# Windowed attention into a mixture of experts on one core: copies of values in their own step, logits of step 13 in a slot's bank, no weight split in steps 10 and 11 and one more in step 13

## The chip, the cores and the metric

The kernel runs on one core of a Trainium2 chip. The metric is the time of one execution on the device in microseconds (us). Five engines work side by side: TensorE (PE, with its weight loads as PEld), VectorE (DVE), ScalarE (ACT), GpSimd (POOL) and SyncE (SP, which issues most DMAs). Each runs its own list of instructions in order; semaphores make one engine wait for another or for a DMA.

## The reference

The attention has 8 batches, 8 heads, 576 positions and 64 values per head, with a causal window of 64. Its output, 4608 rows of 512, goes through a mixture of 8 experts with one expert per row:

```python
scores = scale * np.matmul(q, k.transpose(0, 1, 3, 2))
mask = (rel >= 0) & (rel < 64)            # rel: position of the query less that of the key
attn = softmax(np.where(mask, scores, -1e9))
x = (attn @ v) as rows of 512             # 4608 rows
logits = x @ w_gate + modality_bias[modality_id]
e = argmax(logits); gate = softmax(logits)[e]
out[row] = gate * (relu(x[row] @ w1[e]) @ w2[e])      # w1: 512 x 1024, w2: 1024 x 512
```

Everything is fp32.

## The kernel before, in words

**Steps.** The 4608 rows are 36 pairs of 64-row blocks, 128 rows each. The main loop (line 983) has 36 + 4 steps `s`, and every pair goes through a pipeline of steps. The order of the work is written out by hand: the order of the code is the order of the instructions on every engine, and no scheduler moves anything. In step `s` stand, in this order: `values(s-2)` on PE (attention by values, L635, bank `av`) with `values_out` on DVE (L641 and L643, which makes the rows `xa`); `logits(s-3)` (PE L660 and the addition of the bias on DVE, L665); `scores(s)` (PE L583 into `sp`) with `minima(s)` on DVE (L597); `probs_t(s-1)`, which transposes the softmax on PE (L441) and copies it out on ACT (L618, `pT`); `sums` on POOL (L624); part of the exponentials of pair `s` on ACT (L609); `x_t(s-2)`, the transposition of `xa` (PE L441, then ACT); the heads' transpositions of the next group of queries and keys (`heads_t`, PE L441, copied by DVE or ACT at L548); and in odd steps from 5 on the routing of a group of two pairs (`route2`, `route3`). The routing ends in two scatters of rows on POOL (L736, `xs_scratch<-xa,idx`). While a scatter still reads `xa`, the five buffers of `xa` cannot be written.

**Values.** A pair needs its values twice: `vo` as loaded (SP L499, three buffers) and `ve`, in which the halves are shifted by 64 rows (two buffers). The upper half of `ve[p]` is copied from `vo[p-1]` by DVE (`swap_upper`, L513), the lower half from `vo[p]` by POOL (`swap_v`, L507). Both copies for pair `s-1` are made in step `s`. `values(s-1)` in step `s+1` reads them.

**Experts.** From step `FIRST` = 12 on, work of the mixture of experts is set into the attention: a `gap` is a place in a step at which some matmuls of a slot (256 rows of one expert) are issued. A step has four of them: `first(k, i)` (L280: 12 matmuls into a bank `em` or `sp0`, for the `i`-th half of hidden block `k`) and `second(k, t)` (L302: six matmuls into `y0` or `y1`). Step 12 has a slot's rows and `first(0,0)` and `first(0,1)`; step 13 has `first(1,0)`, `first(1,1)`, `second(0,0)`, `second(0,1)`; step 14 has `first(2,0)`, `first(2,1)`, `second(1,0)`, `second(1,1)`; and so on. After `first(k,1)` ACT makes `hh` (L288) and DVE `hl` (L289), the two parts of the hidden values.

**Weights.** Every matmul of the experts is three: high part by high part, high by low, low by high. The weights of two experts come in 32 pieces of 128 x 512. A call of `weights(s)` (L971) does three things: DVE makes the low part `Wlo` of the piece whose high part was made in the call before (L117), ACT makes the high part `Whi` of the oldest loaded piece (L112), and SP issues the load of another piece (L101 or L105) into one of four buffers `y`. So the low part of the piece with number `n` in the order of the pieces is made three calls after the load, and each call stands in its place of the step. The order is `PIECE_ORDER = (0, 2, 4, 6, 8, 9, 1, 3, 5, 7, 10, ...)`: pieces 0, 2, 4, 6 are what `first(0, .)` and `first(1, .)` need, 8 and 9 what `second(0, .)` needs, 1, 3, 5, 7 the rest of `w1`, 10 and 11 (numbers 10 and 11 in the order) what `second(1, .)` needs. Here `lo3` means the low part of number 3 in the order, and so on. One call stands at the end of each step from `WEIGHTS` = 5 on (L1067). There are two calls more in step 12 (L1041 ahead of `first(0,0)`, and L1056) and in steps 13 to 15 (L1033 and L1056), later one more in odd steps. Nothing but the place in the code and the semaphores keeps a matmul behind its low part; `ready` (L196) refuses only a wrong order of the code.

**Banks.** Transpositions and logits take a PSUM bank from a rotation (`turn_bank`, L485). Before step 12 it has five banks, from then on only the two of `tp`, which are shared by everything that is transposed. The logits of step 12 have bank `y0`, which is still free there (L999).

Of the kernel before, what the change touches and what calls it, by code (L numbers as in the profile page):

```python
# [8 lines left out]
F32 = mybir.dt.float32  # L9
# [10 lines left out]
P = 128  # L20
# [6 lines left out]
def tile_window_attn_moe(  # L27
# [13 lines left out]
    B, H, S, D = q.shape  # L41
# [7 lines left out]
    NPR = NBLK // 2  # L49
# [13 lines left out]
             (12, (0, 2)), (13, (0, 2)), (15, (0, 2)))  # L63
    WEIGHTS = 5
    FIRST = 12


    LATE = ((0, False), (1, True), (0, False), (1, True), (0, True), (1, True))
# [28 lines left out]
    def load_piece(raw, ev, c):  # L97

        if c * WCH < WC:
            ch, f0 = divmod(c * WCH, F)  # L100
            nc.sync.dma_start(  # L101
                out=raw, in_=w1_v[bass.ds(ev, 1), :, ch, f0:f0 + WCH].rearrange("o p f -> (o p) f"))
        else:
            c2 = c - WC // WCH
            nc.sync.dma_start(out=raw, in_=w2_v[bass.ds(ev, 1), :, c2, :].rearrange("o p f -> (o p) f"))  # L105
        return raw

    def split_hi(raw, buf, c):

        if Whi[buf] is None:  # L110
            Whi[buf] = wpool.tile([P, 2 * WC], F32R, name="Whi1")
        nc.scalar.copy(out=Whi[buf][:, c * WCH:(c + 1) * WCH], in_=raw)  # L112

    def split_lo(raw, buf, c):

        cols = slice(c * WCH, (c + 1) * WCH)
        nc.vector.tensor_tensor(  # L117
            out=Wlo[buf][:, cols], in0=raw, in1=Whi[buf][:, cols].bitcast(F32), op=ALU.subtract)
# [8 lines left out]
    def tick(n=1, table=False):  # L127
        for _ in range(n):
            if routing and not table:
                routing.pop(0)()  # L130
            elif queue:
                queue.pop(0)()
                issued[0] += 1
# [98 lines left out]
    def fetch():  # L232
        if fetched:
            return fetched.pop(0)
        row, late, buf, whichever, need = todo.pop(0)
        assert late is not None or not pads
        assert late is None or late in scattered
        tick(need - issued[0], table=True)
        nb = 1 if whichever == NANY else 2
        return dict(xt=load_slot(row, late, nb), buf=buf, any=whichever, nb=nb)  # L240
# [192 lines left out]
    def gap(it, wait=False):  # L433

        if next(it, "end") != "end" and not wait:
            run_later()
            tick()
# [10 lines left out]
    ps_m = actx.enter_context(tc.tile_pool(name="ps_m", bufs=1, space=PSUM))  # L448

    att = actx.enter_context(tc.tile_pool(name="att", bufs=1))  # L450
    work = actx.enter_context(tc.tile_pool(name="work", bufs=1))
# [12 lines left out]
    def by_group(x):  # L464
        return x.rearrange("p (a h j) i -> p a h j i", a=2, h=HP)
# [7 lines left out]
    ve = {}  # L473
# [11 lines left out]
    def turn_bank(s):  # L485

        i = n_tp[0]
        n_tp[0] += 1
        if s < FIRST and i % 5 > 1:
            return ps_m.tile([P, 512], F32, name=("em", "y0", "y1")[i % 5 - 2])  # L490
        return ps_t.tile([P, 512], F32, name="tp")

    def load_v(p):
# [6 lines left out]
        else:  # L500
            for i, g in enumerate((g0, g1)):
                s0 = (g % BPB) * W64
                nc.sync.dma_start(out=t[i * W64:(i + 1) * W64], in_=v_v[g // BPB, s0:s0 + W64])

    def swap_v(p):

        nc.gpsimd.tensor_copy(out=ve[p][0:W64], in_=vo[p][0:W64])  # L507

    def swap_upper(p):
        if p not in ve:  # L510
            ve[p] = work.tile([P, H, D], F32, name="ve", bufs=2)
        if p > 0:
            nc.vector.tensor_copy(out=ve[p][W64:P], in_=vo[p - 1][W64:P])  # L513

# [31 lines left out]
    def heads_out(tp, G, nm, i, copy):  # L546
        dst = by_group(qT if nm == "q" else kT)[:, G % 2, 2 * i:2 * i + 2]
        copy(out=dst.rearrange("p h j (i t) -> p h t (j i)", t=2),  # L548
             in_=tp.rearrange("p (h t i) -> p h t i", h=2, t=2))
# [104 lines left out]
    def logits(p, lt):  # L654
        G, j = divmod(p, GB)
        xaT = st.pop((p, "xT"))
        for c in range(NC1):
            for i in range(2):
                cols = slice(c * P + i * W64, c * P + (i + 1) * W64)
                nc.tensor.matmul(  # L660
                    out=lt[i * W64:(i + 1) * W64, 0:E], lhsT=xaT[:, cols], rhs=wg[:, c, :],
                    start=(c == 0), stop=(c == NC1 - 1))
        if j == 0:
            st[G, "lg"] = small.tile(sh3, F32, name="lg")
        nc.vector.tensor_tensor(  # L665
            out=st[G, "lg"][:, j, :], in0=lt[:, 0:E], in1=bias_sel[:, p, :], op=ALU.add)
# [144 lines left out]
    def when(step, f, *args):  # L811
        at.setdefault(max(step, -1), []).append((f, args))
# [6 lines left out]
    for p in range(NPR):  # L819
        when(p, load_v, p)  # L820
    when(FIRST - 1, lambda: fetched.append(fetch()))
    for G in range(1, NG):
# [148 lines left out]
    def weights(s):  # L971

        if halves:
            split_lo(*halves.pop(0))
        if len(raws) == 2 or raws and not pieces:
            split_hi(*raws[0])
            halves.append(raws.pop(0))
        while pieces and len(raws) < 2:
            x, c = pieces.pop(0)
            raw = epool.tile([P, WCH], F32, name="y", bufs=4)  # L980
            raws.append((load_piece(raw, evs[x], c), x, c))

    for s in range(NPR + 4):
        j = s % GB
        for f, args in at.pop(s, ()):
            f(*args)
        n_tick = 6 if s < FIRST else 5
        n_gap = 0 if s < FIRST else 4
        G = s // GB + 1
        heads = PARTS[j] if G < NG else ()  # L990
        R = (s - 5) // GB if s >= 5 and j == 1 else -1
        if 1 <= s < FIRST:
            swap_upper(s - 1)

        if 2 <= s < NPR + 2:
            values(s - 2)
            values_out(s - 2)
        if 3 <= s < NPR + 3:
            logits(s - 3, turn_bank(s) if s != FIRST else ps_m.tile([P, 512], F32, name="y0"))  # L999
            if (s - 3) % GB == GB - 1:  # L1000
                route1((s - 3) // GB)
        if s < NPR:
            scores(s)
            if s == FIRST:
                gap(it, True)
            minima(s)
            if s == FIRST - 2:
                tick(todo[0][-1] - issued[0], table=True)
        if 1 <= s <= NPR:
            if s == FIRST:  # L1010
                run_later()
            if s >= FIRST:
                swap_upper(s - 1)
            swap_v(s - 1)
            for a in range(2):
                probs_t(s - 1, a, turn_bank(s))
            sums(s - 1)
        if s < NPR:
            exps(s, (0, 1))
        if s == 0:  # L1020
            first_pair(1, (both[:1], both[1:]))
            cast_bias()
        if n_gap > 0 and s != FIRST:
            gap(it, True)
        if 2 <= s < NPR + 2:
            x_t(s - 2, turn_bank(s) if s != FIRST else ps_m.tile([P, 512], F32, name="y0"))
        run_later()
        tick(2)
        if s < NPR:
            exps(s, (2, 3, 4))  # L1030
        if n_gap > 0:
            if FIRST < s < FIRST + 4 or s % 2:
                weights(s)  # L1033
            if s != FIRST:
                gap(it, True)
        if heads:
            tp = turn_bank(s)
            heads_t(G, *heads[0], tp)
            heads_out(tp, G, *heads[0], nc.vector.tensor_copy)
        if s == FIRST:  # L1040
            weights(s)  # L1041
            gap(it, True)
        run_later()
        tick(n_tick)
        cnt = None
        if R >= 0:
            tp = turn_bank(s)
            rk = route2(R, tp)
            if R == NG - 1 or any(R == T for T, _ in EARLY):
                cnt = counts_out(tab if R == NG - 1 else pl, counts(R, tp))  # L1050
            route3(R, rk)
        if s < NPR:
            exps(s, (5, 6, 7))
        if n_gap > 2:
            if FIRST <= s < FIRST + 4:
                weights(s)  # L1056
            gap(it, True)
        if heads:
            tp = turn_bank(s)
            heads_t(G, *heads[1], tp)  # L1060
            heads_out(tp, G, *heads[1], nc.scalar.copy if heads[1] == K1 else nc.vector.tensor_copy)
        run_later()
        tick(n_tick)
        if s == WEIGHTS:
            load_weights()
        if s >= WEIGHTS:
            weights(s)  # L1067
        if n_gap > 3:
            gap(it, True)
        run_later()  # L1070
        if s == 1:
            select_bias()
        if s == 4:
            nc.sync.dma_start(out=xs_blk[DUMMY:DUMMY + 2].rearrange("b p c -> p b c"), in_=padrow)
        for T, xs_ in EARLY:
            if T == R:
                plan(T, xs_, cnt)
# [267 lines left out]
```

## Time and profile before

| | |
|---|---|
| three runs | 634.1, 636.05, 635.59 us |
| their median | 635.59 us |
| the profiled execution's own time | 635.35 us |
| its span | 633.6 us |
| mean granted clock of PE | 0.994 |

The span is the time from the first to the last instruction that the profile shows; the profiled execution's own time is 1.75 us longer. In the profile's lists of instructions a row gives start and duration in us, engine, line, operation, destination and sources (partitions x elements and type), the number of instructions that the row joins, and in brackets how long the engine had stood idle before and what ended that. The tables of waits give for each kind of wait the total in us, how often it occurred, and the longest one. The tables by stretches of time give for each stretch its length, then the busy time and count of PE, PEld, DVE, ACT and POOL.

### The profile page before, as it was taken

The numbers are of one execution on the slowest core, as the hardware profiler recorded it, in microseconds if no ns is written. First come the engines' busy times: TensorE is split into PE (matmuls) and PEld (weight loads), VectorE is DVE, ScalarE is ACT, GpSimd is POOL, SyncE is SP. The second block draws the span as 40 slices with busy tenths as digits, with TensorE's granted clock in tenths as the row PEclk, the third lists the DMA queues.
The fourth block names the chain that finished last, engine by engine and source line by source line (L and its number), as shares of the span: only waits on it lengthen the run. The fifth ranks groups of instructions, "written<-read, shape, count | busy, mean of one in ns | idle before, by whom it ended". The sixth has DMA issues, their size and how long they took to land.

```text
span 633.6 us, 17229 instructions
## 1 busy us (share of the span) xinstructions
PE 617.9 (98%) x6513; PEld 554.1 (87%) x6513; DVE 359.9 (57%) x1449; ACT 299.0 (47%) x933; POOL 136.0 (21%) x315
## 2 busy tenths in 40 slices
PE   8999899999999999999999999999999999999996
PEld 5888789889898889898988898999899989989886
DVE  3899987676777666656644353212314714666511
ACT  3899886757566646555462111111113513554411
POOL 6332412212320320322122221001001101101102
PEclk7999999999999999999999999999999999999999
DMA  9999856676457452544212117302332713677300
GB/s 181 206 245 229 226 143 200 169 185 185 131 141 199 134 151 61 148 136 112 68 52 101 62 73 285 96 21 68 86 114 90 247 64 124 199 242 250 99 8 30
DMA packets 138773, 88.07 MB, mean 139 GB/s; under 512 B 116618, under 2 KB 116672, under 8 KB 138560
## 3 DMA queue, kind: packets, MB, share of 16 engines
q1 hardware_dynamic: 130112, 67.44, 40.4%
q0 software_dynamic: 5888, 18.93, 7.8%
q8 instruction: 52, 0.85, 0.6%
q10 hardware_dynamic: 2688, 0.58, 0.4%
q14 instruction: 33, 0.27, 0.1%
HBM read 67.49 MB, written 23.91 MB: 144 GB/s over the span
## 4 chain that ended last, share of the span: by engine, by line
PE 64%; DVE 0%; ACT 0%; issue 0%; POOL 0%; POOLq 0%; ACTq 0%
PE y L302 26%; PE em L280 16%; PE sp L280 10%; PE tp L441 4%; PE av L635 2%; PE sp L583 2%; PE y L353 1%; PE tp L660 1%; PE em L255 1%; PE tp L255 1%; PE sp L328 0%; PE em L328 0%; DVE xa L643 0%; ACT ss L609 0%; POOL out_dram L366 0%
## 5 line engine op out<-in xcount | busy, mean ns | idle before, releaser
L302 PE MATMUL y<-Whi,hh 128*128 128x512 f32 x288 | 118.7, 412 | 0.0
L609 ACT ACTIVATE ss<-ss,mn 128x128 f32<-128x128 f32 x288 | 112.7, 398 | 2.9 <-DMA y<-in_moe_modality_id_dram 2.2
L302 PE MATMUL y<-Whi,hl 128*128 128x512 f32 x288 | 112.8, 392 | 0.0
L302 PE MATMUL y<-Wlo,hh 128*128 128x512 f32 x288 | 112.7, 391 | 0.0
L280 PE MATMUL em<-xh,Whi 128*128 128x256 f32 x400 | 102.8, 291 | 0.1
L280 PE MATMUL em<-xh,Wlo 128*128 128x256 f32 x400 | 98.0, 279 | 0.0
L289 DVE SCALAR_TENSOR_TENSOR hl<-em,hh 128x512 fp32r<-128x512 f32 x50 | 34.5, 689 | 91.0 <-ACT hh L288 91.0
L313 POOL DMA_INDIRECT out_dram<-y,id x36 | 37.3, 1037 | 221.4 <-DVE y L310 140.1
L280 PEld LDWEIGHTS em<-xh,Whi 128*128 128x128 f32 x400 | 75.4, 189 | 1.3 <-DVE xl L194 0.4
L280 PEld LDWEIGHTS em<-xh,Wlo 128*128 128x128 f32 x400 | 75.3, 188 | 0.9
L288 ACT ACTIVATE hh<-em 128x512 fp32r<-128x512 f32 x50 | 29.6, 592 | 92.8 <-PE em L280 88.8
L597 DVE CUSTOM_DVE_ANT_0 ss<-sp,masks 128x128 f32<-128x128 f32 x288 | 63.6, 285 | 11.3 <-PE sp L583 11.1
L618 ACT COPY pT<-tp 128x512 f32<-128x512 f32 x57 | 31.6, 591 | 72.5 <-PE tp L441 72.3
L302 PEld LDWEIGHTS y<-Whi,hl 128*128 128x128 f32 x288 | 54.1, 188 | 12.3
L280 PE MATMUL em<-xl,Whi 128*128 128x256 f32 x400 | 63.0, 279 | 0.0
L302 PEld LDWEIGHTS y<-Whi,hh 128*128 128x128 f32 x288 | 54.1, 188 | 7.3
L302 PEld LDWEIGHTS y<-Wlo,hh 128*128 128x128 f32 x288 | 54.3, 188 | 7.0
L609 ACT ACTIVATION_READ_ACCUMULATOR ss<-ss,mn 128x1 f32 x288 | 56.2, 195 | 0.0
L736 POOL DMA_INDIRECT xs_scratch<-xa,idx x36 | 36.3, 1009 | 83.1 <-DVE lm L679 27.2
L280 PEld LDWEIGHTS em<-xl,Whi 128*128 128x128 f32 x400 | 53.7, 188 | 0.0
L289 DVE SCALAR_TENSOR_TENSOR hl<-sp,hh 128x512 fp32r<-128x512 f32 x22 | 15.2, 691 | 60.8 <-ACT hh L288 60.8
L288 ACT ACTIVATE hh<-sp 128x512 fp32r<-128x512 f32 x22 | 13.1, 597 | 76.6 <-PE sp L280 76.6
(249 smaller groups left out, 1259.7 us busy)
## 6 DMA issues: line engine op xcount, KB each, us to landing
xt<-xs_scratch SPq DMA_DIRECT2D x18, 514.0 KB, 4.0
vo<-in_v_dram SPq DMA_DIRECT2D x32, 256.0 KB, 3.8
y<-in_moe_w_dram SPq DMA_DIRECT2D x32, 256.0 KB, 3.9
vo<-in_moe_w_dram SPq DMA_DIRECT2D x24, 256.0 KB, 3.7
ss<-in_moe_w_dram SPq DMA_DIRECT2D x24, 256.0 KB, 3.8
xs_scratch<-xs_scratch SPq DMA_DIRECT2D x8, 514.0 KB, 5.8
pT<-in_moe_w_dram SPq DMA_DIRECT2D x16, 256.0 KB, 3.6
qk<-in_k_dram SPq DMA_DIRECT2D x14, 256.0 KB, 5.0
```

The lines of the kernel that those rows point to most:

```text
L255: nc.tensor.transpose(out=tp[:, n * P:(n + 1) * P].bitcast(F32R), in_=xt[:, t, c * P:(c + 1) * P].bitcast(F32R), identity=ident_r)
L280: nc.tensor.matmul(out=hb[:, i * TP:(i + 1) * TP], lhsT=w[buf][:, c0:c0 + P], rhs=x[:, c * TP:(c + 1) * TP], start=(n == 0), stop=(n == le ...
L288: nc.scalar.activation(out=hh, in_=hb, func=AF.Relu),
L289: nc.vector.scalar_tensor_tensor(out=hl, in0=hb, scalar=0.0, in1=hh.bitcast(F32), op0=ALU.max, op1=ALU.subtract)))
L302: nc.tensor.matmul(out=sl["y", t], lhsT=h[:, i * TP + t * P:i * TP + (t + 1) * P], rhs=w[buf][:, c0:c0 + DM], start=(k == 0 and n == 0), s ...
L313: ins = nc.gpsimd.indirect_dma_start(out=out, out_offset=bass.IndirectOffsetOnAxis(ap=sl["id"][:, t:t + 1], axis=0), in_=y, in_offset=None ...
L441: nc.tensor.transpose(out=out_, in_=in_, identity=ident[p0:p0 + n, p0:p0 + n])
L583: nc.tensor.matmul(out=sp[a][c * W64:(c + 1) * W64, hp * P:(hp + 1) * P], lhsT=qT[rows, place(g + c, hp), :], rhs=kT[rows, win(c, hp), :], ...
L597: nc.vector.tensor_tensor_reduce(out=ss[a][:, hp, :], in0=sp[a][:, hp * P:(hp + 1) * P], in1=mask, scale=-1.0 / 8.0, scalar=3.0e38, op0=AL ...
L609: nc.scalar.activation(out=ss[a][:, hp, :], in_=ss[a][:, hp, :], func=AF.Exp, bias=mn[:, h:h + 1], scale=-1.0, accum_out=sm[:, h:h + 1])
L618: nc.scalar.copy(out=pT, in_=pp)
L736: ins = nc.gpsimd.indirect_dma_start(out=xs, out_offset=bass.IndirectOffsetOnAxis(ap=idx[:, j:j + 1], axis=0), in_=xg[j], in_offset=None)
```

## The change

There are three parts.

1. `swap_v` is moved. POOL's copy of the lower half of `ve[s]` now stands in step `s` itself, after the first half of the heads' transpositions and ahead of the routing; it was made in step `s+1` ahead of `probs_t`. `new_ve` allocates the buffer for whichever of the two copies comes first.
2. The logits of step 13 have the bank `y0`, too, instead of one of the two banks `tp`.
3. The calls of `weights` at the ends of steps 10 and 11 are left out (`PAUSE`). The call of step 12 ahead of `first(0,0)` now has its like in step 13, so step 13 has four calls. All pieces behind the third are made two calls later than before in steps 12 and 13, and one call later from the end of step 13 on; the last low part moves from step 25 to step 26.

```diff
@@ constants
     FIRST = 12
+    PAUSE = 10, 11
@@ values
-    def swap_v(p):
-
-        nc.gpsimd.tensor_copy(out=ve[p][0:W64], in_=vo[p][0:W64])
-
-    def swap_upper(p):
+    def new_ve(p):
         if p not in ve:
             ve[p] = work.tile([P, H, D], F32, name="ve", bufs=2)
+
+    def swap_v(p):
+
+        new_ve(p)
+        nc.gpsimd.tensor_copy(out=ve[p][0:W64], in_=vo[p][0:W64])
+
+    def swap_upper(p):
+        new_ve(p)
         if p > 0:
             nc.vector.tensor_copy(out=ve[p][W64:P], in_=vo[p - 1][W64:P])
@@ the main loop, step s
         if 3 <= s < NPR + 3:
-            logits(s - 3, turn_bank(s) if s != FIRST else ps_m.tile([P, 512], F32, name="y0"))
+            logits(s - 3, ps_m.tile([P, 512], F32, name="y0") if FIRST <= s < FIRST + 2 else turn_bank(s))
...
             if s >= FIRST:
                 swap_upper(s - 1)
-            swap_v(s - 1)
+            if s == 1:
+                swap_v(0)
             for a in range(2):
                 probs_t(s - 1, a, turn_bank(s))
...
             heads_out(tp, G, *heads[0], nc.vector.tensor_copy)
+        if FIRST <= s < FIRST + 2:
+            weights(s)
         if s == FIRST:
-            weights(s)
             gap(it, True)
         run_later()
         tick(n_tick)
+        if 1 <= s < NPR:
+            swap_v(s)
         cnt = None
...
-        if s >= WEIGHTS:
+        if s >= WEIGHTS and s not in PAUSE:
             weights(s)
```

On POOL, steps 5 and 6 before, from the copy for pair 4 on: the copy for pair 4, the sums of step 5, the two scatters of the routing in step 5, and then the copy for pair 5 and the sums of step 6.

```order
L507 COPY ve<-vo 64x512
L624 TENSOR_SCALAR rs<-sm 128x8
L735 COPY xa_101<-idc 128x1
L736 DMA xs_scratch<-xa_101,idx 39168x514
L735 COPY xa_102<-idc 128x1
L736 DMA xs_scratch<-xa_102,idx 39168x514
L507 COPY ve<-vo 64x512
L624 TENSOR_SCALAR rs<-sm 128x8
```

The same place after the change (all lines behind the new function are five higher):

```order
L513 COPY ve<-vo 64x512
L629 TENSOR_SCALAR rs<-sm 128x8
L513 COPY ve<-vo 64x512
L740 COPY xa_101<-idc 128x1
L741 DMA xs_scratch<-xa_101,idx 39168x514
L740 COPY xa_102<-idc 128x1
L741 DMA xs_scratch<-xa_102,idx 39168x514
L629 TENSOR_SCALAR rs<-sm 128x8
```

The copy for pair 5 has moved from behind the two scatters to ahead of them.

On PE, `first(0,0)` in step 12 before: four pairs of matmuls by the high and the low part of pieces 0, 2, 4, 6 (numbers 0 to 3), then four by the low part `xl` of the rows. A name with a number is one buffer; `Whi_65` and `Wlo_66` hold the parts of the first expert's weights.

```order
L280 MATMUL em<-xh,Whi_65 128x256 [waits DVE_49]
L280 MATMUL em<-xh,Wlo_66 128x256
L280 MATMUL em<-xh,Whi_65 128x256
L280 MATMUL em<-xh,Wlo_66 128x256
L280 MATMUL em<-xh,Whi_65 128x256
L280 MATMUL em<-xh,Wlo_66 128x256
L280 MATMUL em<-xh,Whi_65 128x256
L280 MATMUL em<-xh,Wlo_66 128x256
L280 MATMUL em<-xl,Whi_65 128x256 x2
L280 MATMUL em<-xl,Whi_65 128x256 [waits DVE_49]
L280 MATMUL em<-xl,Whi_65 128x256
```

The same matmuls after the change:

```order
L281 MATMUL em<-xh,Whi_65 128x256 [waits DVE_49]
L281 MATMUL em<-xh,Wlo_66 128x256
L281 MATMUL em<-xh,Whi_65 128x256
L281 MATMUL em<-xh,Wlo_66 128x256
L281 MATMUL em<-xh,Whi_65 128x256
L281 MATMUL em<-xh,Wlo_66 128x256
L281 MATMUL em<-xh,Whi_65 128x256
L281 MATMUL em<-xh,Wlo_66 128x256 [waits DVE_49]
L281 MATMUL em<-xl,Whi_65 128x256 x4
```

The order is the same; the eighth matmul, by `lo3`, now has a wait of its own for DVE, because `lo3` is made in step 12 itself. It was made at the end of step 10.

On PE, `second(1,0)` in step 14 before, six matmuls into one bank by the parts of pieces 10 and 11:

```order
L302 MATMUL y_2095<-Whi_65,hh 128x512
L302 MATMUL y_2095<-Wlo_66,hh 128x512
L302 MATMUL y_2095<-Whi_65,hl 128x512
L302 MATMUL y_2095<-Whi_65,hh 128x512
L302 MATMUL y_2095<-Wlo_66,hh 128x512 [waits DVE_49]
L302 MATMUL y_2095<-Whi_65,hl 128x512
```

The same six after the change:

```order
L303 MATMUL y_2093<-Whi_65,hh 128x512
L303 MATMUL y_2093<-Wlo_66,hh 128x512 [waits DVE_49]
L303 MATMUL y_2093<-Whi_65,hl 128x512
L303 MATMUL y_2093<-Whi_65,hh 128x512 [waits Activation_49]
L303 MATMUL y_2093<-Wlo_66,hh 128x512 [waits DVE_49]
L303 MATMUL y_2093<-Whi_65,hl 128x512
```

The order is the same again. The fifth matmul, by `lo11`, waited for the first call of step 14 (L1033) before; now it waits for the second one (L1056 before, `weights` ahead of the third gap), because `lo11` comes a call later. The second matmul waits for `lo10` of the first call and the fourth for ACT's high part of piece 11, made in that call.

More of the change, by code (lines that the diff above doesn't have):

```diff
@@ L503, in load_v @@
                 nc.sync.dma_start(out=t[i * W64:(i + 1) * W64], in_=v_v[g // BPB, s0:s0 + W64])
+    def new_ve(p):
+        if p not in ve:
+            ve[p] = work.tile([P, H, D], F32, name="ve", bufs=2)
     def swap_v(p):
+        new_ve(p)
         nc.gpsimd.tensor_copy(out=ve[p][0:W64], in_=vo[p][0:W64])
     def swap_upper(p):
-        if p not in ve:
-            ve[p] = work.tile([P, H, D], F32, name="ve", bufs=2)
+        new_ve(p)
         if p > 0:
```

## The prediction

> **What bounds the kernel now.** First the page: its first part for the engines, its second for where in the span they are busy.
>
> ```profile
> span 633.6 us, 17229 instructions
> PE 617.9 (98%) x6513; PEld 554.1 (87%) x6513; DVE 359.9 (57%) x1449; ACT 299.0 (47%) x933; POOL 136.0 (21%) x315
> PE   8999899999999999999999999999999999999996
> DVE  3899987676777666656644353212314714666511
> PEclk7999999999999999999999999999999999999999
> ```
>
> PE bounds the span: it is busy for 98% of it, and only 15.7 us (633.6 - 617.9) are left, part of them at the start and the end. The change adds no matmul and removes none, so it can gain only idle time of PE. The table of waits, PE's rows, names what there is:
>
> ```profile
> PE av L635 <- POOL ve L507: 2.5, 4, 0.8
> PE tp L441 <- DVE lg L665: 1.9, 3, 1.0
> PE tp L441 <- DVE xa L643: 1.5, 1, 1.5
> ```
>
> The three parts of the change aim at these three rows: 5.9 us together. But a wait that goes is a gain only if nothing else is late by then, and the second digit row shows DVE at 0.8 to 0.9 of its time in slices 2 to 5 (16 to 80 us). So I looked at what DVE waits for from step 4 to step 13, in the timeline and in one stretch:
>
> ```profile
> 31.63 0.29 DVE L597 CUSTOM_DVE_ANT_0 ss<-sp,masks 128x128 f32<-128x128 f32 x1 [0.24 <-PE sp L583]
> 46.60 0.69 DVE L643 TENSOR_TENSOR xa<-av,rs 128x512 f32<-128x512 f32 x1 [0.74 <-DMA xs_scratch<-xa,idx]
> 31.63:82.66 51.03, 46.84 (x865) 42.02 (x863) 48.15 (x269) 48.26 (x190) 18.72 (x36) 1.00 0.88 225
> ```
>
> In these 51 us DVE is busy for 48.15 us and ACT for 48.26 us, more than PE (46.84 us). Behind the 0.24 us on PE at 31.63 DVE's only longer wait is the 0.74 us on a scatter. Here DVE sets the pace, and PE's waits are what DVE leaves over.
>
> **Part 1, the copy of values.** The four waits of PE for POOL's copy:
>
> ```profile
> 23.99 0.27 PE L635 MATMUL av<-ve,pT 128*64 128x64 f32 x1 [0.83 <-POOL ve L507]
> 44.40 0.27 PE L635 MATMUL av<-ve,pT 128*64 128x64 f32 x1 [0.75 <-POOL ve L507]
> 55.05 0.27 PE L635 MATMUL av<-ve,pT 128*64 128x64 f32 x1 [0.46 <-POOL ve L507]
> 66.52 0.27 PE L635 MATMUL av<-ve,pT 128*64 128x64 f32 x1 [0.47 <-POOL ve L507]
> 36.91 0.23 POOL L624 TENSOR_SCALAR rs<-sm 128x8 f32<-128x8 f32 x1 [4.08 <-ACT ss L609]
> 41.15 1.10 POOL L736 DMA_INDIRECT xs_scratch<-xa,idx  x1 [3.76 <-issue]
> ```
>
> All four go: the copy no longer stands behind two scatters, and POOL has 3.76 us free ahead of them. The last three lie in the stretch of DVE; PE would only reach DVE's next product sooner, so I cost them at 0. The first one, in step 3, lies before it, where DVE waits for PE. Everything from there on comes up to 0.83 us earlier: bounds 0 and 0.83, taken 0.83.
>
> **Part 3, the steps without a split.** These are the rows around the end of step 11 and the start of step 12:
>
> ```profile
> 69.40 0.69 DVE L117 TENSOR_TENSOR Wlo<-y,Whi 128x512 fp32r<-128x512 f32 x1
> 70.13 0.42 DVE L513 COPY ve<-vo 64x512 f32<-64x512 f32 x1
> 71.62 0.65 PE L441 MATMUL tp<-ident_r,xa 128*128 128x128 f32 x4 [1.47 <-DVE xa L643]
> 75.33 1.10 PE L583 MATMUL sp<-kT,qT 64*64 64x128 f32 x32
> 75.12 0.68 DVE L117 TENSOR_TENSOR Wlo<-y,Whi 128x512 fp32r<-128x512 f32 x1
> 75.72 0.19 DVE L641 RECIPROCAL rs<-rs 128x8 f32<-128x8 f32 x1
> 80.25 0.28 PE L280 MATMUL em<-xh,Wlo 128*128 128x256 f32 x1
> 81.35 0.68 DVE L117 TENSOR_TENSOR Wlo<-y,Whi 128x512 fp32r<-128x512 f32 x1
> ```
>
> Two splits leave DVE ahead of step 12: 70.13 - 69.40 = 0.73 and 75.72 - 75.12 = 0.60 us. With part 1, DVE is 0.83 + 0.73 = 1.56 us earlier by the scores of step 12, which start at 73.77 in place of 75.33, and 0.83 + 0.73 + 0.60 = 2.16 us earlier by its own list behind them. The minima can't run ahead of the scores, so between 1.56 and 2.16 I take 1.65.
>
> But a new wait stands there. The eighth matmul of `first(0,0)` needs `lo3`, which was made in step 10; now the first split of step 12 makes it, at the place of the row 81.35. It starts at 81.35 - 1.65 = 79.70 and ends at 80.38, and PE follows at about 80.45. Before, this matmul ran at 80.25. So the gain of 1.65 us that PE brings into step 12 is used up there, and 0.2 us more: **+0.2 by the eighth matmul**, whatever came before. (If part 1 brings nothing in step 3, DVE is 0.83 later, and it is +1.0.)
>
> **Part 2, the logits of step 13.** The transpositions of `probs_t` in step 13:
>
> ```profile
> 85.31 0.66 PE L441 MATMUL tp<-ident_r,ss 128*128 128x128 f32 x4
> 86.93 0.66 PE L441 MATMUL tp<-ident_r,ss 128*128 128x128 f32 x4 [0.97 <-DVE lg L665]
> 87.34 0.36 PE L280 MATMUL em<-xh,Whi 128*128 128x256 f32 x1
> ```
>
> From the first four to `first(1,0)` it is 87.34 - 85.31 = 2.03 us. Without the logits in a `tp` bank the second four follow the first directly. Four of them hold PE until the next instruction for 87.34 - 86.93 = 0.41 us, so eight take 0.82, say 0.85 us: a gain of 1.18. Its bounds are 0.97, the wait itself, and 1.2. No other reader of a `tp` bank is late there by the timeline. **-1.2**, so that PE stands at 0.2 - 1.2 = -1.0 from step 13 on. The extra split of step 13 (0.68 us of DVE) lies in waits of DVE for PE of 1 us.
>
> **Part 3 again, in step 14.** The fifth matmul of `second(1,0)` needs `lo11`, which the first call of step 14 made; now the second call does.
>
> ```profile
> 99.66 0.68 DVE L117 TENSOR_TENSOR Wlo<-y,Whi 128x512 fp32r<-128x512 f32 x1
> 102.00 0.69 DVE L548 COPY kT<-tp 128x512 f32<-128x512 f32 x1 [0.79 <-PE tp L441]
> 102.98 0.69 DVE L289 SCALAR_TENSOR_TENSOR hl<-em,hh 128x512 fp32r<-128x512 f32 x1 [0.29 <-ACT hh L288]
> 104.51 0.68 DVE L117 TENSOR_TENSOR Wlo<-y,Whi 128x512 fp32r<-128x512 f32 x1
> 101.71 0.48 PE L302 MATMUL y<-Whi,hh 128*128 128x512 f32 x1
> 102.73 0.39 PE L302 MATMUL y<-Wlo,hh 128*128 128x512 f32 x1
> 94.62:105.11 10.49, 10.49 (x138) 9.45 (x137) 8.16 (x41) 5.92 (x23) 2.85 (x4) 1.00 0.63 178
> ```
>
> PE runs `second(1,0)` from 101.71 and its fifth matmul at 102.73. `lo10` (now at 99.66) is in time. `lo11` is not: it now stands at 104.51, behind the copy of `kT`, `hl` and five small instructions of the routing, and ends at 105.19. With a little for the release PE waits from 102.73 to about 105.25: **+2.5 us**. DVE can't catch up by being ahead, since in this step it waits for PE at 102.00, and at 102.98 for ACT, whose `hh` follows PE too. Queued behind the waiting matmul is all of PE's list. In the stretch of step 14 PE is busy for 10.49 of 10.49 us, so nothing absorbs it. The bounds are 0, were the copy of `kT`, `hl` and the routing (102.00 to 104.51, 2.5 us) not ahead of it, and 2.9, with the longest split on record, below. I take 2.5.
>
> **Behind step 14** every split is one call later than before. In the order of the later steps I found no matmul that needs its low part sooner than that. The last low part moves to the end of step 26, and DVE's next instructions have room ahead of them:
>
> ```profile
> 236.50 0.69 DVE L643 TENSOR_TENSOR xa<-av,rs 128x512 f32<-128x512 f32 x1 [1.15 <-PE av L635]
> ```
>
> 0.68 us of split fits into 1.15 us. Cost 0, and at most 0.7 without that cover.
>
> **The sum:** +0.2 - 1.2 + 2.5 = +1.5 us on the profiled execution's 635.35: 636.85. The median of the three runs, 635.59, is 0.24 above that execution; between 636.85 and 637.09 I say **637.0 us**.
>
> **A rule against the change.** Splits of DVE and copies of POOL meet in the trace:
>
> ```profile
> 89.01 0.60 POOL L507 COPY ve<-vo 64x512 f32<-64x512 f32 x1 [5.54 <-DMA vo<-in_v_dram]
> 89.05 1.11 DVE L117 TENSOR_TENSOR Wlo<-y,Whi 128x512 fp32r<-128x512 f32 x1
> 80.03 0.76 POOL L507 COPY ve<-vo 64x512 f32<-64x512 f32 x1 [0.35 <-DMA vo<-in_v_dram]
> ```
>
> The split under a copy took 1.11 us, the ones without 0.68: 0.43 us more. The Trainium skill, "GPSIMD Engine Reference", section Specifications, says that GpSimd shares its SBUF interfaces with VectorE and that there is contention with VectorE instructions that have two SBUF inputs, as a split has; the trace agrees, by the 1.11 against 0.68. What matters is that the copy at 80.03 waits for its load, so that in step 12 it runs between about 78.4 (80.03 - 1.65) and 80.8, across `lo3` (79.70 to 80.38).
>
> **The rivals.**
>
> *Fewer waits than I count (A).* The wait in step 14 doesn't come or is short, because DVE gets to the second split before the copy of `kT`. Against it: the order of DVE is fixed, and 102.00 waits for PE. Time: 635.35 + 0.2 - 1.2 = 634.4. Chance 0.15.
>
> *Neither new wait (B).* DVE gets all 2.16 us ahead, more at the place of `lo3`, and PE keeps its 1.65 into step 13: 635.35 - 1.65 - 1.2 = 632.5. Chance 0.08. Speaks against it: two waits that did not stand in the list before.
>
> *The copies meet the splits (C), slower.* In step 3 nothing is gained, since DVE doesn't follow, and `lo3` is stretched by a copy: 636.85 + 0.83 + 0.43 = 638.1. It decides from the point where POOL's copy in step 12 starts later than 79.1 (79.70 - 0.60). Chance 0.13.
>
> *The clock drops (D), slower.* PE idle early on is followed by a lower clock:
>
> ```profile
> 6.00:8.00 2.00, 1.01 (x10) 0.57 (x8) 0.16 (x1) 0.00 (x0) 1.71 (x15) 1.00 1.31 262
> 8.00:10.00 2.00, 1.27 (x25) 1.25 (x28) 1.30 (x7) 0.72 (x2) 1.78 (x11) 0.62 1.27 205
> 10.00:12.00 2.00, 2.00 (x28) 1.67 (x21) 1.07 (x11) 0.74 (x4) 0.45 (x3) 0.50 1.20 211
> 12.00:14.00 2.00, 2.00 (x14) 1.88 (x13) 1.79 (x12) 1.44 (x8) 0.17 (x1) 0.50 1.29 234
> 14.00:16.00 2.00, 2.00 (x36) 1.50 (x35) 1.79 (x9) 2.00 (x11) 0.86 (x2) 0.68 0.99 220
> ```
>
> PE stood idle for 1.72 of the 4 us from 6 to 10, and over 8 to 16 us it lost 2 x (0.38 + 0.50 + 0.50 + 0.32) = 3.4 us of full clock. If the 2.5 us in step 14 do the same: 636.85 + 3.4 = 640.3. Against it: the longest wait of later steps, 1.47 at 71.62, left the clock of its stretch at 1.00, and here PE is full on both sides. The Trainium skill, "TensorE: Matmul & The Clock Gate", Part 1, halves the clock after an idle window of about 3.4 us; by that rule a wait of 2.5 us keeps it. Chance 0.08.
>
> **How the numbers follow.** 0.56 is left for my sum, with a range of its own of 636.0 (part 2 and the minima at their best, the wait in step 14 at 2.0) to 638.0 (`lo3` stretched, or step 3 without gain). A measurement of this kernel can tell about 0.3%, 1.9 us, from no change: 633.7 and 637.5 around 635.59. About a quarter of my own case lies over 637.5 (0.14); with C and D slower has 0.35. A and the rest, 0.57, are the same. Faster has B, 0.08. The range takes in A, my case and C, from 634.2 to 638.6, and leaves out B and D, 0.16.
>
> **What would show it.** In the profile after: no row `av <- ve` among PE's waits; no `tp <- lg` in step 13; the eighth matmul of `first(0,0)` with a wait on `Wlo` ending between 80.2 and 80.9; the fifth of `second(1,0)` with one of 2 to 2.7 us on `Wlo`, at a clock of 1.00. It is wrong if there is no wait in step 14, or if PE's idle time is over 2 us away from 15.7 + 1.5.

## The result, and the profile after

| | before | after |
|---|---|---|
| median | 635.68 us (17 runs, 634.1 to 636.93) | 638.81 us (17 runs, 635.71 to 640.76) |
| profiled execution, span | 633.6 us | 637.4 us |
| PE busy | 617.9 us | 619.8 us |
| PE not busy (span less busy) | 15.7 us | 17.6 us |

The ratio is 1.0052 (95% interval 1.0043 to 1.0061): 3.3 us slower. The forecast was 637.0, 1.3 us slower, in a range up to 638.6, and "within 0.3%" had the larger chance. So the sign of the sum was right and its size was not, and the median lies just outside the range.

The page of the kernel after, its engines and the row of PE's clock:

```profile
span 637.4 us, 17230 instructions
PE 619.8 (97%) x6513; PEld 555.5 (87%) x6513; DVE 359.6 (56%) x1449; ACT 299.5 (47%) x933; POOL 135.3 (21%) x315
PEclk7999998999999999999999999999999999999999
```

PE executes the same 6513 matmuls. Its idle time grew by 1.9 us (15.7 to 17.6; the sum said 1.5), but its busy time grew by 1.9 us, too, with no matmul more. The clock row says where: the seventh digit (96 to 112 us) is an 8. The waits of PE after:

```profile
PE y L303 <- DVE Wlo L118: 2.2, 1, 2.2
PE em L281 <- DVE Wlo L118: 1.6, 1, 1.6
PE tp L442 <- DVE xa L648: 1.5, 2, 1.0
PE y L442 <- DVE xa L648: 1.4, 2, 0.8
PE em L855 <- DVE hh L850: 1.3, 1, 1.3
PE tp L442 <- DVE lg L670: 1.2, 2, 0.8
```

The row `av <- ve` is gone, and so is the wait on `lg` in step 13; the two waits on `lg` that are left lie elsewhere. The row on `hh` stands in before, too. The two new rows on `Wlo` are the two places that the prediction named. Here they are in PE's timeline, with the splits that they wait for in DVE's:

```profile
80.42 0.39 PE L281 MATMUL em<-xh,Wlo 128*128 128x256 f32 x1 [1.58 <-DVE Wlo L118]
104.34 0.80 PE L303 MATMUL y<-Wlo,hh 128*128 128x512 f32 x1 [2.24 <-DVE Wlo L118]
104.93 0.63 PE L303 MATMUL y<-Whi,hl 128*128 128x512 f32 x1
```

```profile
79.68 0.68 DVE L118 TENSOR_TENSOR Wlo<-y,Whi 128x512 fp32r<-128x512 f32 x1
101.09 0.69 DVE L553 COPY kT<-tp 128x512 f32<-128x512 f32 x1 [0.79 <-PE tp L442]
102.08 0.69 DVE L290 SCALAR_TENSOR_TENSOR hl<-em,hh 128x512 fp32r<-128x512 f32 x1 [0.30 <-ACT hh L289]
103.61 0.68 DVE L118 TENSOR_TENSOR Wlo<-y,Whi 128x512 fp32r<-128x512 f32 x1
```

The split `lo3` was forecast from 79.70 to 80.38 with PE at 80.45; it stands at 79.68, and PE starts at 80.42. In step 14 DVE waits 0.79 and 0.30 us as before, and PE waits 2.24 us for `lo11`. What the sum did not have is behind that wait: the matmul at 104.93 takes 0.63 us, where its like of before took 0.39. The table by stretches (busy time and count of PE, PEld, DVE, ACT, POOL, then PE's granted clock, DMA share, GB/s):

```profile
102.00:104.00 2.00, 0.10 (x1) 0.00 (x0) 1.78 (x7) 1.16 (x7) 0.70 (x2) 1.00 0.35 132
104.00:106.00 2.00, 1.66 (x6) 1.37 (x7) 1.30 (x5) 0.76 (x3) 0.23 (x1) 0.52 0.27 10
106.00:108.00 2.00, 2.00 (x8) 1.59 (x7) 0.00 (x0) 1.12 (x2) 0.00 (x0) 0.63 0.92 293
108.00:110.00 2.00, 2.00 (x58) 1.69 (x60) 0.48 (x1) 0.00 (x0) 0.00 (x0) 1.00 1.12 346
```

From 104 to 108 us the clock is 0.52 and 0.63: rival D, to which 0.08 was given. The loss is 2 x (0.48 + 0.37) = 1.7 us of full clock, half of the 3.4 us that D was priced at. How far PE is behind or ahead at the start of each step's `values` matmuls (first `av` row of the step, in the timelines of the two profiled executions):

| step | before | after | difference |
|---|---|---|---|
| 2 | 17.96 | 17.79 | -0.17 |
| 3 | 23.99 | 22.73 | -1.26 |
| 7 | 44.40 | 42.32 | -2.08 |
| 8 | 49.38 | 48.34 | -1.04 |
| 12 | 73.20 | 71.63 | -1.57 |
| 13 | 82.77 | 83.05 | +0.28 |
| 14 | 94.62 | 93.72 | -0.90 |
| 15 | 105.11 | 108.29 | +3.18 |
| 26 | 224.79 | 228.16 | +3.37 |

Steps 12 and 13 are as worked out: +1.85 in step 12, which holds the wait of the eighth matmul (forecast 1.65 + 0.2), and -1.18 in step 13. Step 14 costs 4.08 us in place of 2.5. That was one execution; the theory to be tested was this. The two new waits cost what the sum says, and the idle PE then loses its clock for some us in a part of the executions. The rival: the clock has another cause, or the extra time comes from other terms of the sum that one execution can't show.

### The profile page after: what moved, and what is told of

Its sections match the earlier page's. It is cut to its first block, busy times and chain, and to the rows that moved or that the text cites. A ratio compares the mean times of both kernels' runs of the same rounds, so it can differ in the third digit from the quotient of the medians.

```text
span 637.4 us, 17230 instructions
## 1 busy us (share of the span) xinstructions
PE 619.8 (97%) x6513; PEld 555.5 (87%) x6513; DVE 359.6 (56%) x1449; ACT 299.5 (47%) x933; POOL 135.3 (21%) x315
## 4 chain that ended last, share of the span: by engine, by line
PE 64%; DVE 0%; ACT 0%; issue 0%; POOL 0%; POOLq 0%; ACTq 0%
PE y L303 26%; PE em L281 16%; PE sp L281 10%; PE tp L442 4%; PE av L640 2%; PE sp L588 2%; PE y L354 1%; PE tp L665 1%; PE em L256 1%; PE tp L256 1%; PE sp L329 0%; PE em L329 0%; DVE xa L648 0%; ACT ss L614 0%; POOL out_dram L367 0%
```

## The experiments

All ratios are to the kernel before on the same chip, five rounds, with the 95% interval. The medians of before were 635.7 to 637.3 us on the chips used, so 0.1% is 0.64 us.

| run | what it is | ratio | interval |
|---|---|---|---|
| after_again | the changed kernel | 1.0059 | 1.0044 to 1.0073 |
| after_third | the changed kernel | 1.0042 | 1.0027 to 1.0057 |
| filled_both | both new waits filled with matmuls | 1.0039 | 1.0026 to 1.0053 |
| filled_both_2 | the same again | 1.0041 | 1.0025 to 1.0058 |
| filled_9 | only the wait of step 14 filled | 1.0039 | 1.0023 to 1.0055 |
| no_wait_14 | only the wait on `lo3` | 1.0013 | 0.9997 to 1.0029 |
| wait_14_alone | before, with the wait on `lo11` alone | 1.0060 | 1.0038 to 1.0081 |
| wait_14_again | the same again | 1.0066 | 1.0053 to 1.0079 |
| alone_filled | the same, the wait filled | 1.0042 | 1.0029 to 1.0054 |
| part_1 | the copies alone | 1.0001 | 0.9990 to 1.0013 |
| part_2 | the logits alone | 0.9978 | 0.9964 to 0.9992 |
| part_3 | the splits alone | 1.0051 | 1.0036 to 1.0065 |
| parts_1_2 | the copies and the logits | 0.9982 | 0.9971 to 0.9993 |
| pause_11 | no split left out in step 10 | 0.9954 | 0.9941 to 0.9966 |
| pause_11_2 | the same again | 0.9986 | 0.9973 to 0.9998 |
| pause_10 | no split left out in step 11 | 0.9989 | 0.9966 to 1.0012 |
| part_1_own_xa | the copies, a free buffer in step 7 | 1.0019 | 1.0000 to 1.0037 |
| before_own_xa | before, a free buffer in step 7 | 0.9992 | 0.9979 to 1.0005 |

### The wait in step 14, with and without the rest

no_wait_14, the changed kernel with one call more:

```diff
         if s >= WEIGHTS and s not in PAUSE:
             weights(s)
+        if s == FIRST + 1:
+            weights(s)
```

> The changed kernel with one more call of weights at the end of step 13, so that lo11 is again made in the first call of step 14; lo3 is still made in step 12. Theory (the wait in step 14 costs its 2.24 us and then 1.84 us of half clock): both go, the clock stays at 1.00 around 105 us, and the span is 637.4 - 4.1 = 633.3. Rival (the slow matmuls behind the wait have another cause): only the 2.24 us go, span 635.2.

Taking the wait of step 14 away takes the ratio from 1.0052 to 1.0013, 2.5 us (the two are separate measurements, each against before). It is not the 4.1 us of the theory, and the kernel is not faster than before. In its profiled execution the clock falls behind the other wait, that on `lo3`, from 80 to 88 us; besides that, what is left costs more than the sum says, which is taken up below.

wait_14_alone, the kernel before with one call less:

```diff
-            if FIRST < s < FIRST + 4 or s % 2:
+            if s != FIRST + 2 and (FIRST < s < FIRST + 4 or s % 2):
                 weights(s)
```

> The kernel before with nothing changed but the first call of weights in step 14 left out, so that lo11 is made behind the routing as in the changed kernel. Theory: a wait of about 2.5 us at the fifth matmul of second(1,0) and behind it a granted clock near 0.5 for 3 to 4 us: 4.0 to 4.5 us slower than before. Rival (the clock or another cost comes from another part of the change): the wait alone, 2.5 us slower.

> wait_14_alone once more, beside alone_filled on the same chip. Theory: 2.3 us of wait and, in most executions, about 1.8 us of lost clock: 3.5 to 4 us slower than before. Rival (the wait alone): 2.3 us slower.

1.0060 and 1.0066, 3.8 and 4.2 us: this one wait costs as much as the whole change; the intervals overlap. The two profiled executions of this one kernel differ in what we need. In wait_14_alone, PE's fifth matmul and a later one of the same form, and the stretches behind:

```profile
106.53 0.50 PE L302 MATMUL y<-Wlo,hh 128*128 128x512 f32 x1 [2.26 <-DVE Wlo L117]
...
108.32 0.63 PE L302 MATMUL y<-Wlo,hh 128*128 128x512 f32 x1
```

```profile
106.00:108.00 2.00, 1.47 (x7) 1.34 (x8) 1.50 (x5) 0.96 (x4) 0.23 (x1) 0.79 0.06 10
108.00:110.00 2.00, 2.00 (x6) 1.55 (x6) 0.00 (x0) 1.12 (x2) 0.00 (x0) 0.50 0.87 275
110.00:112.00 2.00, 2.00 (x50) 1.42 (x48) 0.19 (x1) 0.00 (x0) 0.32 (x2) 0.86 1.12 352
```

In wait_14_again the same:

```profile
104.33 0.50 PE L302 MATMUL y<-Wlo,hh 128*128 128x512 f32 x1 [2.26 <-DVE e_used L140]
...
105.57 0.39 PE L302 MATMUL y<-Wlo,hh 128*128 128x512 f32 x1
```

```profile
104.00:106.00 2.00, 1.68 (x9) 1.45 (x10) 1.28 (x5) 1.21 (x4) 0.23 (x1) 1.00 0.21 8
106.00:108.00 2.00, 2.00 (x44) 1.55 (x44) 0.00 (x0) 0.66 (x2) 0.00 (x0) 1.00 0.82 265
```

The wait is 2.26 us in both. (The second is put down to a small DVE instruction right behind the split, which started at 103.59.) In one the clock falls to 0.50 and a matmul takes 0.63 us, in the other it stays at 1.00 and it takes 0.39. From the `values` of step 14 to those of step 15 the one takes 14.56 us (96.02 to 110.58), the other 13.01 (93.82 to 106.83), and before took 10.49. So the wait alone costs 2.52 us, which is the sum's 2.5, and the clock, where it falls, 1.55 more. It fell behind this place in 3 of the 6 profiled executions that had the wait unfilled (after, wait_14_alone and part_3; not in wait_14_again, after_again and after_third). Step 14 took 14.57, 14.56 and 14.46 us in the first three, and 13.01, 13.11 and 13.10 in the others.

### Keeping PE at work in the waits

alone_filled, filled_9 and filled_both add matmuls whose result nobody reads, ahead of the matmul that waits. This is the edit for the wait of step 14; filled_both has six more such matmuls ahead of the eighth of `first(0,0)`:

```diff
             for n, (h, w, i) in enumerate(mm):
+                if n == 4 and k == 1 and t == 0 and position[0] == 6:
+                    sp = ps_s.tile([P, 512], F32, name="sp0")
+                    for _ in range(9):
+                        nc.tensor.matmul(out=sp, lhsT=Whi[buf][:, 0:P], rhs=hi, start=True, stop=True)
                 c0 = WC + (2 * k + i) * DM
```

> wait_14_alone with nine matmuls whose result nobody reads ahead of the fifth matmul of second(1,0), so that PE works while lo11 is late and nothing else changes. Theory (idle PE costs the clock): 2.3 to 2.6 us slower than before, 1.2 to 1.8 us faster than wait_14_again, and the granted clock at 1.00 behind the place. Rival (the time behind the wait has another cause): the same time as wait_14_again.

> The changed kernel with nine more matmuls of 128x512 (about 0.23 us each) into the bank sp0, whose result nobody reads, ahead of the fifth matmul of second(1,0): PE works while it would wait. Theory: the wait shrinks from 2.24 to about 0.2 us, the end of the wait stays where it was (the split is no earlier), the clock stays at 1.00, and the span is 1.8 us shorter than that of the changed kernel, 635.6. Rival (the 1.84 us aren't the idle PE's doing): the span stays at 637.4.

> The changed kernel with PE kept at work in both new waits, by matmuls whose result nobody reads: six ahead of the eighth matmul of first(0,0) and nine ahead of the fifth of second(1,0). The low parts come no earlier, so both places last as long as before. Theory (idle PE costs the clock): about 1.5 to 2 us shorter than the changed kernel, 1.0025 of before, and no stretch of half clock behind the two places. Rival (the idle time alone counts): the same time as the changed kernel.

> filled_both once more. Theory: 1.0035 to 1.004 of before, 1.3 us below after_third. Rival: level with it.

> The changed kernel itself, beside filled_both on the same chip. Theory: about 1.005 of the time of before, the waits on lo3 (1.6 us) and on lo11 (2.2 us) as in the profile after, and half clock behind one or both of them in a part of the executions, so that its times spread over more than 3 us. Rival: the half clock was an accident of one execution and the extra 3.3 us come from elsewhere.

> The changed kernel a third time, beside filled_both_2. Theory: 1.005 to 1.006 of before, 1.3 us (0.2%) above filled_both_2. Rival (the clock costs nothing on the mean): level with filled_both_2.

In filled_both both waits are short, and its clock is 1.00 behind both places:

```profile
83.45 0.38 PE L285 MATMUL em<-xh,Wlo 128*128 128x256 f32 x1 [0.17 <-DVE Wlo L118]
107.38 0.50 PE L311 MATMUL y<-Wlo,hh 128*128 128x512 f32 x1 [0.16 <-DVE Wlo L118]
```

In after_again, the same chip and the same set of runs, the clock falls at the other wait, that on `lo3`:

```profile
82.31 0.38 PE L281 MATMUL em<-xh,Wlo 128*128 128x256 f32 x1 [1.57 <-DVE Wlo L118]
```

```profile
82.00:84.00 2.00, 1.69 (x9) 1.69 (x10) 1.61 (x7) 1.83 (x9) 0.26 (x1) 0.65 0.23 59
84.00:86.00 2.00, 2.00 (x11) 2.00 (x10) 0.55 (x1) 1.12 (x2) 0.00 (x0) 0.50 0.72 215
```

In after_third the clock falls there, too. So in each of the four profiled executions that had both waits unfilled it fell behind exactly one of them: step 14 in after and part_3, `lo3` in after_again and after_third. Behind the filled waits it stayed at 1.00 in all four profiled executions. There step 14 takes 13.00 to 13.13 us, as long as where the clock stayed without filling, so the added matmuls cost nothing in this place.

filled_both missed its 1.0025, and filled_9 its span of 635.6: the profiled execution of filled_9 has 638.5. The clock is 1.00 behind step 14, but in step 7 DVE waits 2.60 us for a scatter, and from 46 to 52 us the clock falls there.

On the mean of all executions the effect is small. alone_filled is 1.0042 against 1.0066 on the same chip (1.5 us), filled_both 1.0039 against 1.0059 (1.3 us), filled_both_2 1.0041 against 1.0042 (nothing). The intervals of the first pair hardly overlap, those of the second do, and the third pair is level, as its rival had it. So that the clock falls, and what it costs then, is shown; how much of the changed kernel's 3.3 us it is on the mean is between nothing and 1.5 us and stays open. The mean granted clock over the executions of each kernel does not settle it. It is 0.9963 in alone_filled against 0.9932 in wait_14_again, and 0.9941 in filled_both_2 against 0.9907 in after_third, but 0.9927 in filled_both against 0.9945 in after_again. These means hold other falls, too: 11 of the 20 profiled executions have one at the start of the kernel, before and after among them.

What filled_both and filled_both_2 agree on is the other share: with PE at work in both waits, the change still costs 1.0039 and 1.0041, 2.5 us (1.6 to 3.7 by the intervals). The sum had 1.5.

### Part by part

part_1, part_2 and part_3 make one part each; parts_1_2 leaves out the third.

> Part 1 alone: POOL's copies in their own step. Theory: PE's four waits on ve go; the 0.83 us of step 3 are kept by DVE up to step 12, 0.8 us faster than before, 0.9987. Rival (the time comes back as waits on xa, since DVE sets the pace): the same as before, 1.000.

> Part 2 alone: the logits of step 13 in y0. Theory: PE's wait on lg in step 13 goes and nothing takes its place, 1.0 to 1.2 us faster than before, 0.9982. Rival (the transpositions then wait for another reader of their bank): the same as before.

> Part 3 alone: no split at the ends of steps 10 and 11, four calls in step 13, copies and logits as before. Theory: the eighth matmul of first(0,0) ends 1.0 us later than before (0.2 with the 0.83 us of part 1 missing), 2.2 us of wait in step 14, and 1.5 to 2 us of lost clock on the mean: 4.7 to 5.2 us slower, 1.0075 to 1.008. Rival (the losses come from all three parts together): as slow as the changed kernel, 1.0052, or less.

> Parts 1 and 2 alone: no step without a split and no fourth call in step 13. Theory: 0.8 us of step 3 and 1.2 us of step 13, 2.0 us faster than before, 0.9968. Rival (part 1 brings nothing, since DVE sets the pace from step 4 on): 1.2 us faster, 0.998.

Part 2 is 1.4 us faster alone, as worked out (1.2). parts_1_2, at 0.9982, is no faster than part 2 alone, as its rival had it. Part 3 alone is as slow as the whole change, 1.0051, and not the 1.0075 to 1.008 expected. These are all the waits of PE in part_3 from 72 to 130 us:

```profile
PE y L303 <- DVE Wlo L118: 2.2, 1, 2.2
PE em L281 <- DVE Wlo L118: 1.6, 1, 1.6
PE tp L442 <- ACT pT L619: 1.0, 1, 1.0
PE y L661 <- DVE se L723: 0.4, 1, 0.4
PE em L281 <- DVE xl L195: 0.3, 1, 0.3
```

Both waits on `Wlo` are there, and there is none on `lg` in step 13, though the logits still have a `tp` bank.

Part 1 brings nothing: 1.0001 (0.9990 to 1.0013). Its four waits on `ve` (2.5 us) are gone from PE's waits, and these are the rows of part_1 on `xa` up to 110 us:

```profile
PE tp L442 <- DVE xa L648: 2.1, 2, 1.6
PE y L442 <- DVE xa L648: 1.2, 2, 0.7
PE em L442 <- DVE xa L648: 0.7, 1, 0.7
```

They are 4.0 us, and before had 1.5: PE waits the same 2.5 us more for `xa`. In DVE's timeline of part_1, step 7 shows it first; the scatter that holds the buffer is in POOL's:

```profile
46.69 0.69 DVE L648 TENSOR_TENSOR xa<-av,rs 128x512 f32<-128x512 f32 x1 [1.56 <-PE y L442]
```

```profile
40.23 1.11 POOL L741 DMA_INDIRECT xs_scratch<-xa,idx  x1 [3.21 <-issue]
```

Before, the scatter was issued at 41.15 and DVE got the buffer at 46.60, after 5.45 us. In part_1 it is issued 0.92 us earlier, and DVE gets the buffer at 46.69, after 6.46. (The matmuls named as the releaser had long been done; in before the same wait is put to the scatter.) PE's lead of 0.91 us in step 3 (step 2 to step 3: 5.12 us in place of 6.03) is 0.36 in step 8. How much is lost there differs between executions: from step 3 to step 8 PE takes 25.39 to 25.58 us in the six profiled executions without part 1, and 25.42 to 26.60 in eleven of the twelve with it (28.39 in filled_9, where the clock fell). The two kernels below are not counted.

To tell whether it is this transfer, step 7 was given a buffer of its own, with part 1 and in before:

```diff
-        xa = st[p, "xa"] = xas[p % XBUF]
+        xa = st[p, "xa"] = xas[p % XBUF] if p != 5 else epool.tile([P, 2, ROW], F32, name="xt")[:, 0]
```

> Part 1 alone, and the rows of pair 5 (step 7) go into the tile xt, which is idle until step 11, so that DVE waits for no scatter there. Theory (the scatter's transfer eats part 1's gain): DVE's wait in step 7 goes, PE stands 0.9 us ahead of before_own_xa from step 8 to step 11 where part_1 stood at 0.4 us ahead of before, and it is 0.5 to 0.9 us faster than before_own_xa. Rival (the gain is lost elsewhere): no faster than before_own_xa.

> The kernel before with that edit alone. Theory: DVE's 0.74 us of step 7 go, 0 to 0.7 us faster than before. Rival: the next buffer is as late, and nothing changes.

The expectation failed: with part 1 it is 1.0019, without 0.9992, so part 1 is not faster there, but slower, by 1.7 us. The profiled execution, at 634.64 us one of the fastest of its 12, shows where the lead goes. The wait in step 7 is gone, and from step 3 to step 9 PE takes 29.92 us, where before took 31.06: here the gain is kept, and more. Then comes this, in DVE's and PE's timelines, two steps later:

```profile
56.62 0.69 DVE L648 TENSOR_TENSOR xa<-av,rs 128x512 f32<-128x512 f32 x1 [2.34 <-DMA xs_scratch<-xa,idx]
```

```profile
57.36 0.68 PE L442 MATMUL em<-ident_r,xa 128*128 128x128 f32 x4 [2.26 <-DVE xa L648]
```

The stretch from 31.63 to 72 us of the same kernel:

```profile
31.63:72.00 40.37, 36.60 (x704) 32.99 (x699) 36.16 (x208) 37.17 (x148) 14.12 (x27) 0.96 0.93 232
```

The next scatter holds the next buffer, for 2.34 us, and from 58 to 62 us the clock falls again. The clock's mean over the 12 executions fits that: 0.9922, against 0.9964 in before_own_xa, 2.7 us of full clock. So in these two executions the lead of part 1 is lost at a scatter, in step 7 or, where that one is out of the way, in step 9. The DMA engines are at a share of 0.93 in this stretch (0.89 in before). That the transfers as a whole bound these steps is what the share suggests; it was not tried with less to transfer, and stays argued.

### Without the two new waits

pause_11 and pause_10 are the changed kernel with `PAUSE = 11,` or `PAUSE = 10,`: every piece is one call earlier, and neither matmul waits for its low part.

> The changed kernel with PAUSE = 11 alone: lo3 is made in step 10 again and every piece from there on is one call earlier, lo11 in the first call of step 14. Theory: neither new wait. PE keeps about 0.9 us into step 12 (0.83 of step 3; the split of step 10 is back, so PE's wait on xa in step 11 stays near 1.47) and gains 1.18 in step 13: 2.1 us faster than before, span 631.5. Rival (the earlier steps gain nothing, since DVE sets their pace): only step 13's 1.2 us, span 632.4.

> pause_11 once more on another chip: neither new wait. Theory: 1.2 us of part 2 and 0.3 to 1.5 us that the earlier steps keep, 0.9955 to 0.998 of before. Rival (0.9954 was an accident of that chip): no faster than part_2.

> The changed kernel with PAUSE = 10 alone: lo3 is made at the end of step 11, lo11 in the first call of step 14. Theory: neither new wait, and the split that goes in step 10 is the one ahead of xa, so that PE's wait on xa in step 11 shrinks from 1.47 to about 0.7 and the 1.56 us are kept into step 12; with 1.18 in step 13 it is 2.7 us faster than before, 0.9957. Rival (lo3 at the end of step 11 holds up the minima of step 12): no better than pause_11.

pause_11 is 0.9954 on one chip and 0.9986 on another: faster than before both times, by 0.9 to 2.9 us. The second was measured beside part 2 alone (0.9978) and is no better than it. pause_10 misses its 0.9957; its 12 runs go from 633.56 to 641.71 us. Even pause_11 had a fall of the clock in its profiled execution, at the old wait on `xa` in step 11:

```profile
70.73 0.99 PE L442 MATMUL tp<-ident_r,xa 128*128 128x128 f32 x4 [1.87 <-DVE xa L648]
```

```profile
72.00:74.00 2.00, 2.00 (x19) 1.61 (x18) 1.58 (x9) 2.00 (x10) 0.00 (x0) 0.50 1.18 321
```

## Why the prediction was wrong, point by point

Two steps of it failed: the clock, which the sum put at nothing, and the lead of step 3, which the sum took as kept. The first is the miss of the profiled execution, the second shows in the medians of the kernels with filled waits. The forecast's signs say the same. Both waits came at their places and with their lengths, the two old rows went, and PE's idle time was 0.4 us from the 17.2 forecast; only "at a clock of 1.00" failed. A sign on idle time could not see it, since slower matmuls count as busy.

- **The wait in step 14, +2.5.** Right: 2.24 us of wait, and 2.52 us from step to step where the clock stayed (wait_14_again).
- **The logits of step 13, -1.2.** Right: -1.18 in the trace after, 0.9978 alone. But part 3 takes the same wait away by being late: in part_3, without part 2, PE has no wait on `lg` in step 13 either, and the step is as short. Beside part 3, part 2 brought nothing more in these traces, and the whole change is as slow as part 3.
- **The clock (rival D).** This step failed: the sum had 0 for it. The mechanism was priced and given 0.08, because 1.47 us of waiting had left the clock alone in the stretch before. The rule cited there from the Trainium skill, "TensorE: Matmul & The Clock Gate", Part 1, spoke against it, too. In the profiled execution it came, at 1.7 us of full clock in place of 3.4, and step 14 took 14.57 us where it took 13.10 in after_third, where the clock stayed. Together with the 2.5 us it makes the 4.08 us of step 14. Its share of the mean is the 0 to 1.5 us above.
- **The eighth matmul, +0.2.** In the profiled execution this held: PE came into step 12 with a lead of 1.57 us (0.17 of it from step 2), and the matmul ran at 80.42, where before had 80.25. On the mean it did not. "Everything from there on comes up to 0.83 us earlier: bounds 0 and 0.83, taken 0.83" let the lead of step 3 run through to step 12. Part 1 alone measures 1.0001, and its trace is only 0.27 us ahead at step 12. So for the mean the case in brackets, +1.0, is the nearer one; this is worked out from part 1 alone, and not measured at the matmul itself. The row of the stretch that I quoted ended in a DMA share of 0.88, and DVE's only longer wait there was on a scatter. I read from that row that DVE set the pace, and let the scatter come earlier with everything else.
- **Behind step 14, 0.** It is 0.2: from step 25 to 26 the lag grows from 3.16 to 3.37, and PE's wait on `lg` there is 0.80 in place of 0.59. Every profiled kernel in which the last low part comes a call later has it, and no other.
- With +1.0 and 0.2, the sum is +1.0 - 1.2 + 2.5 + 0.2 = 2.5 us, which is what the kernels with filled waits measure. Their intervals begin at 1.6 us, so the 1.5 of the forecast lies just outside them, and the agreement is no finer than that.
- **The copies meet the splits (rival C).** Its result, 638.1, was near the median, by luck: the clock is not in it. Half of its reason held on the mean: little is kept of step 3. The other half did not: POOL's copy in step 12 ran at 77.65, before the point of 79.1 that the rival named, and `lo3` took 0.68 us, not 1.11.

## What to carry to other kernels

When a wait goes, ask of every wait that comes after it whether its releaser comes earlier, too: an engine does, a transfer need not (here one issued 0.92 us earlier came no earlier). The share of DMA in a stretch is to be read beside the engines' busy times. Work that is put off to ease one engine has a last date at each of its readers; look for the reader whose producer is queued behind something that itself waits for the reader's engine, since such a wait can't be made up. A wait of some 2 us on TensorE can cost 1.5 us beyond itself, in some executions and not in others. So set the profile of one execution against several runs.

## What the runs showed of the hardware that was not expected

The granted clock falls behind waits of PE that are shorter than thought. Single waits of 2.24 and 2.26 us were followed by it in some executions and not in others, and one of 1.87 us (pause_11) was, too. The wait of 1.57 or 1.58 us on `lo3` was followed by it in after_again, after_third and no_wait_14, where waits of 0.92 to 1.10 and 0.3 us came shortly ahead of it. It was not in after, part_3 and filled_9; in part_3 and filled_9 such a wait stood ahead of it, too.

What a fall takes is a multiple of nearly the same amount: 2 x (0.48 + 0.37) = 1.7 us of full clock in after, 2 x (0.21 + 0.50 + 0.14) = 1.7 in wait_14_alone, 2 x (0.35 + 0.50) = 1.7 in after_again, and twice that, 3.4, at the start of before and behind the wait on `lo3` in no_wait_14, and three times that, 5.1, at the start of after_again. At half clock 1.7 us are lost in 3.4 us. The fall at the start, in 11 of 20 profiled executions, came in kernels with parts of the change and without. The kernels with part 1 reach step 3 at 22.73 to 23.95 us with it and at 21.11 to 21.95 without it.

The Trainium skill, "TensorE: Matmul & The Clock Gate", Part 1, has a freely running window of about 3.4 us, and half clock after an idle one. The length of a fall and the chance in it agree with such a window. That a whole window must be idle does not: a wait of 1.87 us was enough.

On three of the chips PE waited another 0.4 to 1.6 us in step 12, for ACT's copies behind the slot's rows (the row `tp <- pT` above). It did so with the change and without it: wait_14_alone, which is the kernel before up to step 13, has 1.5 us. What holds the rows there was not tried.
